# A token-mixing product made from seven products of quarters, in two passes

## The chip, the cores and the metric

One core of one Trainium2 chip runs the whole kernel in one launch. The metric is the device time of that launch in microseconds (us), the median of three runs. A profiled execution gives the trace that the numbers below come from; its own time stands beside its span.

## The reference

```python
def _A_ref(x, wqkv, wo):                 # S=2048, D=512, 32 heads of 16
    q, k, v = ...                        # x @ wqkv, cut in heads
    scores = jnp.einsum("bhqd,bhkd->bhqk", q, k) * scale
    o = jnp.einsum("bhqk,bhkd->bhqd", _softmax(scores), v)
    return o.transpose(0, 2, 1, 3).reshape(B, S, D) @ wo

def _B_ref(x, w_in, w_sp, b_sp, w_out):  # Fh=688
    z = _gelu(jnp.einsum("bsd,df->bsf", x, w_in))
    z1 = z[..., :Fh]
    z2 = _layernorm(z[..., Fh:], axis=-1)
    g = jnp.einsum("ts,bsf->btf", w_sp, z2) + b_sp[None, :, None]
    return jnp.einsum("bsf,fd->bsd", z1 * g, w_out)

h = x + _A_ref(_layernorm(x, axis=-1), A_wqkv, A_wo)
h2 = h + _B_ref(_layernorm(h, axis=-1), B_w_in, B_w_sp, B_b_sp, B_w_out)
```

The change is about `w_sp @ z2`, a 2048 x 2048 matrix by a 2048 x 688 one, and what surrounds it.

## The kernel before

All data are fp32. Every product is made from two parts of each operand, a rounded high part and the rest, both in a reduced fp32 format (`F32R`): `split` (L74-81) makes them, the high part by a copy on ScalarE (ACT), VectorE (DVE) or GpSimd (POOL), the low part by a subtraction on DVE or POOL, and `mm3` (L83-86) issues three matmuls, high by high, high by low, low by high. S is cut into NB = 16 row blocks of 128, the 688 columns of z1 and z2 into two halves of FC = 344, and the 688 rows of w_out into six blocks (five of 128, one of 48).

There are four stages.

1. Up to about 190 us: layer norm, the projection to q, k and v, and their stores.
2. Up to 1422 us: attention, as a loop over 512 units (`units`, L644), whose order on each engine is written by hand. In some units `load_weights` (L629-642) loads a piece of wo or w_in and splits it on POOL. The last units already start the next stage for the first row blocks (`load_o`, `split_o`, `make_h`, L693-698).
3. The middle stage, up to 1594.7 us, in which a scheduler orders the instructions. Per row block: `load_o` (L540) loads the attention's result and scales it on POOL, `split_o` (L554) splits it, `make_h` (L559) multiplies it by wo, adds x, stores h in DRAM and normalises it into `hn` (L573, DVE); `turn` (L724) transposes `hn` into `hT`; `make_z` (L733) makes z1 and z2 by 48 matmuls with w_in, gelu on ACT (L745), stores z1 in DRAM (L748, on SyncE's queue, SP), normalises z2 (L752, DVE) and splits it into the resident operand `z2`, which holds all 16 blocks.
4. The last stage, also ordered by the scheduler. `load_ws` (L709) loads the next row of w_sp blocks (1 MB) and splits it on ACT and DVE. `gate` (L789) makes one row block of g, two halves of 16 x 3 matmuls of 344 columns, then adds b_sp and multiplies by z1 (L803, DVE). `finish` (L807) transposes that product in six blocks (L814), copies them out of PSUM as two parts in groups of two, three and one (`pT`), multiplies by w_out's parts `wu` in 18 matmuls of 512 columns, adds h (L823) and stores the output (L824). `finish` of a block stands behind `gate` of the next one. `load_wu` (L781) loads w_out at the stage's start and splits it on POOL.

SBUF memory comes from pools; tiles with one tag and `bufs=n` share n places, so a new tile waits for the last reader of the one whose place it takes. PSUM has four accumulators `g`, two `acc` and one tile `tp` in the last stage.

Of the kernel before, what the change touches and what calls it, by code (L numbers as in the profile page):

```python
# [18 lines left out]
P = 128  # L19
# [7 lines left out]
NB = S // P  # L27
NQ = S // 512
# [15 lines left out]
def block_kernel(ctx: ExitStack, tc: tile.TileContext, x, wqkv, wo, w_in, w_sp4, b_sp, w_out, out):  # L44
# [26 lines left out]
    z_scr = dram.tile([S, FH], F32, name="z_scr")  # L71
# [458 lines left out]
    wc = ctx.enter_context(tc.tile_pool(name="wc", bufs=3))  # L530
    early = ctx.enter_context(ExitStack())
    ec = early.enter_context(tc.tile_pool(name="early_c", bufs=1))
    e2 = early.enter_context(tc.tile_pool(name="early_2", bufs=2))
    wo2 = [wc.tile([P, DB, D], F32R, name=f"wo{i}", tag="w8") for i in range(2)]
# [24 lines left out]
    def make_h(sb, acc):  # L559
# [12 lines left out]
        hns[sb] = e2.tile([P, D], F32, name="hn")  # L572
        nc.vector.tensor_scalar(hns[sb], h, mv[:, 0:1], rs, op0=ALU.subtract, op1=ALU.mult)  # L573

    with ExitStack() as at:
# [53 lines left out]
        def load_weights(i):  # L629

            t = wc.tile([P, DB * D], F32, name="wg", tag="w8")
# [10 lines left out]
            split(dst[0][:, a, f], dst[1][:, a, f], t, "pool", "pool")  # L642

        units = [(hg, qb, kb) for hg in range(HG) for qb in range(NQ) for kb in range(NB)]  # L644
        prev, turn, later = None, [0], []
        with tc.manual_schedule(engines={E.PE, E.Activation, E.DVE, E.SP}):
            for n in range(0, len(units), 2):
# [43 lines left out]
                if n % 32 == 16 and n < 6 * 32:  # L691
                    load_weights(n // 32)
                if n in (498, 502, 506):  # L693
                    load_o((n - 498) // 4)
                if n in (502, 506):
                    split_o((n - 502) // 4)
                if n in (504, 508):
                    make_h((n - 504) // 4, later[0].tile([P, 512], F32, name="h"))
# [5 lines left out]

    zc = ctx.enter_context(tc.tile_pool(name="zc", bufs=1, side="right"))
    z2 = [zc.tile([P, NB, FH], F32R, name=f"z2{i}") for i in range(2)]
    wsp = [wc]

    def load_ws(tb):  # L709
        pool = wsp[tb % 2]  # L710
        t = pool.tile([P, NB, P], F32, name="wt", tag="w8")
        nc.sync.dma_start(t, w_sp4[tb])
        ws = [pool.tile([P, NB, P], F32R, name=f"ws{i}", tag="w8") for i in range(2)]
        for k in range(2):
            b = slice(k * NB // 2, (k + 1) * NB // 2)
            split(ws[0][:, b, :], ws[1][:, b, :], t[:, b, :], "act")
        return ws

    with ExitStack() as mid:
        m2 = mid.enter_context(tc.tile_pool(name="mid_2", bufs=2))  # L720
        ps = mid.enter_context(tc.tile_pool(name="mid_ps", bufs=5, space=PSUM))
# [11 lines left out]
        def make_z(sb):  # L733
            hT = hTs.pop(sb)
            z = [m2.tile([P, FH], F32, name=f"z{i}") for i in range(2)]
            st = m2.tile([P, 2, 6], F32, name="zst")
            for i in (1, 0):
                for c in range(2):
# [12 lines left out]
            rs = rstd_of(m2, mv[:, 1:2], 1)  # L751
            nc.vector.tensor_scalar(z[1], z[1], mv[:, 0:1], rs, op0=ALU.subtract, op1=ALU.mult)  # L752
# [3 lines left out]
        turn(0)  # L756
        split_o(2)
        for sb in range(NB):
            if sb + 2 < NB:
                make_h(sb + 2, ps.tile([P, 512], F32, name="acc"))  # L760
            if sb + 3 < NB:
                load_o(sb + 3)
                split_o(sb + 3)
            if sb + 1 < NB:
                turn(sb + 1)
            if sb == NB - 2:
                ws = load_ws(0)
            make_z(sb)
# [3 lines left out]
    with ExitStack() as fin:  # L772
        fc_ = fin.enter_context(tc.tile_pool(name="fin_c", bufs=1))
        f2 = fin.enter_context(tc.tile_pool(name="fin_2", bufs=2))
        wsp.append(fin.enter_context(tc.tile_pool(name="fin_w", bufs=3)))
# [3 lines left out]
        wu = [fc_.tile([P, len(FB), D], F32R, name=f"wu{i}") for i in range(2)]  # L779

        def load_wu():  # L781
            t = f2.tile([P, len(FB), D], F32, name="wg", bufs=1)
            nb, fn = len(FB) - 1, FB[-1][1]
            nc.sync.dma_start(t[:, :nb, :], w_out[:nb * P, :].rearrange("(a p) c -> p a c", p=P))
            nc.sync.dma_start(t[:fn, nb, :], w_out[nb * P:, :])
            for i, (_, n) in enumerate(FB):
                split(wu[0][:n, i, :], wu[1][:n, i, :], t[:n, i, :], "pool", "pool")

        def gate(tb, ws):  # L789

            rows = slice(tb * P, (tb + 1) * P)
            z1 = f2.tile([P, FH], F32, name="z1")
            nc.sync.dma_start(z1, z_scr[rows, :])
            g = [ps_g.tile([P, 512], F32, name="g") for i in range(2)]
            for i in range(2):
                f = slice(i * FC, (i + 1) * FC)
                for sb in range(NB):
                    mm3(g[i][:, :FC], ws[0][:, sb, :], ws[1][:, sb, :],
                        z2[0][:, sb, f], z2[1][:, sb, f], sb == 0, sb == NB - 1)
            pr = f2.tile([P, FH], F32, name="pr")  # L800
            for i in range(2):
                f = slice(i * FC, (i + 1) * FC)
                nc.vector.scalar_tensor_tensor(pr[:, f], g[i][:, :FC], bias[:, tb:tb + 1], z1[:, f],  # L803
                                               op0=ALU.add, op1=ALU.mult)
            return pr

        def finish(tb, pr):  # L807
            rows = slice(tb * P, (tb + 1) * P)
            h = f2.tile([P, D], F32, name="h")
            nc.sync.dma_start(h, h_scr[rows, :])  # L810
            pT = [f2.tile([P, len(FB), P], F32R, name=f"pT{i}") for i in range(2)]
            tp = ps_t.tile([P, 8, P], F32, name="tp")
            for i, (f0, fn) in enumerate(FB):
                nc.tensor.transpose(tp[:fn, i, :], pr[:, f0:f0 + fn], ident)  # L814
                if i in (1, 4, 5):
                    b = slice({1: 0, 4: 2, 5: 5}[i], i + 1)
                    split(pT[0][:fn, b, :], pT[1][:fn, b, :], tp[:fn, b, :], "act")
            acc = ps_o.tile([P, 512], F32, name="acc")
            for i, (f0, fn) in enumerate(FB):
                mm3(acc, pT[0][:fn, i, :], pT[1][:fn, i, :],  # L820
                    wu[0][:fn, i, :], wu[1][:fn, i, :], i == 0, i == len(FB) - 1)
            y = f2.tile([P, D], F32, name="y")
            nc.vector.tensor_add(y, acc, h)  # L823
            nc.sync.dma_start(out[rows, :], y)  # L824

        prev = None
        for tb in range(NB):
            nxt = load_ws(tb + 1) if tb + 1 < NB else None
            if tb == 0:
                load_wu()  # L830
            pr = gate(tb, ws)
            if prev is not None:
                finish(tb - 1, prev)
            prev, ws = pr, nxt
        finish(NB - 1, prev)


# [27 lines left out]
```

## Time and profile before

| what | us |
|---|---|
| median of three runs | 1930.77 |
| the runs | 1930.58, 1931.93, 1930.77 |
| the profiled execution's own time | 1930.47 |
| its span, from the first to the last instruction | 1928.7 |

The granted TensorE clock of that execution is 0.998 of full speed over the span. In the profile, PE is TensorE's matmuls and PEld its weight loads; a line number is that of the kernel before; a row of a group has the instructions' count, their busy time and the mean duration in ns, then the engine's idle time ahead of them and what ended it. A row of a stretch has its window, its length, and the busy time and number of instructions of each engine in it, then the clock granted, the busy share of the DMA engines and GB/s. A row of the timeline has the start in us and the duration.

### The profile page before, as it was taken

To read this page: it belongs to the slowest core of one execution; us is meant where nothing else is said; L and a number is where in the kernel's file an instruction comes from. 1 tells how busy PE (TensorE), PEld (TensorE's weight loads), DVE (VectorE), ACT (ScalarE), POOL (GpSimd) and SP (SyncE) were. 2 spreads that over 40 slices of the span, in tenths; PEclk is the share of its full clock that TensorE was granted. 3 is DMA by queue.
4 is the path that set the end of the run, shared out by engine and by line. 5 is a ranking of instruction groups with operands and counts; after the bars stand their busy time and mean duration, and the time that the engine had idled before them with its cause. 6 is when DMAs were issued, how large, how long until landed. Compare 5 with 4: busy or idle time off the path is not lost.

```text
span 1928.7 us, 31977 instructions
## 1 busy us (share of the span) xinstructions
PE 1911.9 (99%) x11800; PEld 1094.2 (57%) x11800; DVE 1444.7 (75%) x2886; ACT 1261.6 (65%) x1590; POOL 139.7 (7%) x201
## 2 busy tenths in 40 slices
PE   9999999999999999999999999999999999999999
PEld 6765444444444344444444444444369999989987
DVE  6487999999999999999999999999358773232231
ACT  3335888888888888888888888888943331111110
POOL 2130000101011000000000000000012222000000
PEclk9999999999999999999999999999999999999999
DMA  5777111211221120111021021000143334232210
GB/s 187 194 190 175 40 24 32 71 24 28 50 53 49 38 40 22 31 37 24 24 53 24 13 51 37 13 13 6 29 118 118 109 119 175 81 109 92 81 66 34
DMA packets 121845, 128.90 MB, mean 67 GB/s; under 512 B 60248, under 2 KB 80744, under 8 KB 118104
## 3 DMA queue, kind: packets, MB, share of 16 engines
q1 hardware_dynamic: 121656, 126.84, 24.4%
q8 instruction: 93, 1.52, 0.3%
q14 instruction: 64, 0.52, 0.1%
q0 software_dynamic: 32, 0.01, 0.0%
HBM read 84.32 MB, written 41.55 MB: 65 GB/s over the span
## 4 chain that ended last, share of the span: by engine, by line
PE 93%; DVE 2%; DMA 1%; ACT 1%; SPq 1%; issue 1%; POOL 0%; ACTq 0%; POOLq 0%; DVEq 0%
PE pv L604 25%; PE m L200 25%; PE s L593 12%; PE acc L84 6%; PE acc L86 5%; PE acc L85 5%; PE g L85 4%; PE g L84 4%; PE g L86 4%; PE tp L814 1%; ACT pt L596 0%; DMA rc<-r_scr 0%; DVE rs_t L101 0%; DMA xr<-in_x 0%; SPq L547 0%
## 5 line engine op out<-in xcount | busy, mean ns | idle before, releaser
L596 ACT ACTIVATE pt<-s 128x1024 f32<-128x1024 f32 x1024 | 993.2, 1030 | 144.5 <-PE s L593 140.5
L205 DVE TENSOR_REDUCE mx<-m 128x1 f32<-128x512 f32 x1511 | 958.7, 684 | 105.2 <-PE m L200 64.7
L200 PE MATMUL m<-kst,qst 48*128 48x512 f32 x1511 | 607.1, 448 | 0.0
L604 PE MATMUL pv<-pt,vst 128*32 128x512 f32 x4096 | 550.7, 605 | 0.4 <-ACT o L611 0.4
L593 PE MATMUL s<-qst,kst 50*128 50x512 f32 x2048 | 465.6, 428 | 2.6 <-ACT pt L596 2.0
L200 PEld LDWEIGHTS m<-kst,qst 48*128 48x128 f32 x1511 | 263.2, 184 | 315.8 <-DVE mx L205 221.7
L593 PEld LDWEIGHTS s<-qst,kst 50*128 50x128 f32 x2048 | 223.2, 185 | 56.8 <-ACT pt L596 32.4
L200 PE MATMUL m<-uvs,qst 48*128 48x512 f32 x503 | 249.0, 496 | 0.0
L200 PEld LDWEIGHTS m<-uvs,qst 48*128 48x128 f32 x503 | 91.8, 183 | 207.3 <-DVE mx L205 205.3
L214 DVE CUSTOM_DVE_ANT_0 ab<-m,ab 128x512 f32<-128x512 f32 x252 | 171.6, 681 | 3.7 <-ACT ab L210 2.0
L604 PEld LDWEIGHTS pv<-pt,vst 128*32 128x32 f32 x4096 | 82.9, 108 | 160.9 <-issue 155.1
L76 ACT ACTIVATE ws<-wt 128x1024 fp32r<-128x1024 f32 x32 | 33.6, 1055 | 210.8 <-PE g L85 203.6
L84 PE MATMUL g<-z,ws 128*128 128x344 f32 x512 | 165.2, 323 | 0.6 <-issue 0.6
L85 PE MATMUL g<-z,ws 128*128 128x344 f32 x512 | 164.7, 322 | 0.0
L86 PE MATMUL g<-z,ws 128*128 128x344 f32 x512 | 163.4, 319 | 0.0
L210 ACT ACTIVATE ab<-m 128x512 f32<-128x512 f32 x251 | 151.0, 602 | 16.7 <-PE m L200 16.3
L803 DVE SCALAR_TENSOR_TENSOR pr<-g,bias,z 128x344 f32<-128x344 f32 x32 | 18.4, 576 | 182.3 <-PE g L86 180.3
L85 PEld LDWEIGHTS g<-z,ws 128*128 128x128 f32 x512 | 96.2, 188 | 5.8 <-issue 5.2
L84 PEld LDWEIGHTS g<-z,ws 128*128 128x128 f32 x512 | 96.2, 188 | 0.9 <-issue 0.9
L86 PEld LDWEIGHTS g<-z,ws 128*128 128x128 f32 x512 | 96.2, 188 | 0.6
L84 PE MATMUL acc<-wi,hT 128*128 128x344 f32 x256 | 83.7, 327 | 0.0
L86 PE MATMUL acc<-wi,hT 128*128 128x344 f32 x256 | 82.4, 322 | 0.0
(136 smaller groups left out, 1603.7 us busy)
## 6 DMA issues: line engine op xcount, KB each, us to landing
wt<-in_w_sp SPq DMA_DIRECT2D x16, 1024.0 KB
qst<-q_scr SPq DMA_DIRECT2D x192, 64.0 KB
kst<-k_scr SPq DMA_DIRECT2D x48, 256.0 KB
k_scr<-part SPq DMA_DIRECT2D x16, 512.0 KB
q_scr<-part SPq DMA_DIRECT2D x16, 512.0 KB
z_scr<-z SPq DMA_DIRECT2D x16, 344.0 KB
z<-z_scr SPq DMA_DIRECT2D x16, 344.0 KB
xg<-in_x SPq DMA_DIRECT2D x16, 256.0 KB
```

The source lines that it names most:

```text
L76: nc.scalar.activation(hi, src, AF.Copy)
L84: nc.tensor.matmul(ps, lh, rh, start=first, stop=False)
L85: nc.tensor.matmul(ps, lh, rl, start=False, stop=False)
L86: nc.tensor.matmul(ps, ll, rh, start=False, stop=last)
L200: nc.tensor.matmul(acc, q[r, p, c], keys[r, p], start=True, stop=True)
L205: nc.vector.reduce_max(at(t, e if t else e - 1), acc, axis=AX.X)
L210: nc.scalar.activation(ab[0], acc, AF.Abs)
L214: nc.vector.tensor_tensor_reduce(ab[0], acc, ab[0], 0.5, LOW, ALU.add, ALU.max, at(0, 0))
L593: nc.tensor.matmul(s[:, t, :], k[r, p, kb * P:(kb + 1) * P], q[r, p, :], start=True, stop=True)
L596: nc.scalar.activation(t, s, AF.Exp, scale=DH ** -0.5)
L604: nc.tensor.matmul(pv[0][32 * j:32 * j + 32, :], vst[hg % 2][:, c:c + 32], pts[j % 2][:, j // 2, :], start=kb == 0, stop=kb == NB - 1)
L814: nc.tensor.transpose(tp[:fn, i, :], pr[:, f0:f0 + fn], ident)
```

## The change

Write w_sp as quarters a11, a12, a21, a22 of eight by eight blocks and z2 as b11, b12, b21, b22 (eight row blocks by 344 columns). In place of eight products of quarters there are seven, on sums and differences:

- s1 = a21 + a22, s2 = s1 - a11, s3 = a11 - a21, s4 = a12 - s2
- t1 = b12 - b11, t2 = b22 - t1, t3 = b22 - b12, n4 = b21 - t2 (as the code has them)
- pass 1: g7 = s3 t3, g6 = s2 t2, g4 = a22 n4, g5 = s1 t1; pass 2: g1 = a11 b11, g3 = s4 b22, g2 = a12 b21

Pass 1 goes over p = 0 to 7, one row of blocks of the upper and the lower half of w_sp at a time. `rows_of_a` loads a11, a21 and a22 of row p, makes the sums on DVE and stores s2; `put` makes the parts; the four products follow; their sums q0, q1, q2 go to DRAM (`g_scr`). It also makes b11's parts, and in its last step those of b22 and b21 and of the first operands of pass 2. Pass 2 goes over p again, with its order on TensorE, ACT and DVE written by hand: three products, which with q give row blocks p (`top`) and p + 8 (`bot`); their transposes, products with w_out and stores stand between the halves of the products. All six transposes of a block are issued ahead of their copies, except for the last block. `fetch` loads what the next step needs.

The operands t3, t2, n4 and t1 are made in the middle stage, on POOL for seven pairs of row blocks and on DVE and ACT for the last; so the row blocks are taken in the order 0, 1, 8, 9, 2, 10, ..., 7, 15. z2 is now stored too, both stores on ACT's queue, and `hn` and z2 are normalised on ACT (`normal`) with a small DVE operation ahead of it.

w_out's parts are made by POOL in six units of the attention (`split_wu`) and stored (`store_wu`); the last step of pass 1 loads them in the places of n4.

The diff, cut:

```diff
+    h_rows = [0, 1, HB, HB + 1] + [sb + HB * i for sb in range(2, HB) for i in range(2)]
...
+    def normal(out, z, mv, rs, pool):
+        nb = pool.tile([P, 1], F32, name="nb")
+        nc.vector.tensor_scalar(nb, rs, mv[:, 0:1], -1.0, op0=ALU.mult, op1=ALU.mult)
+        nc.scalar.activation(out, z, AF.Identity, bias=nb, scale=rs)
...
+        def split_wu(i):
+            f0, fn = FB[i]
+            t = e2.tile([P, D], F32, name="wu", tag="hn", bufs=3)
+            nc.sync.dma_start(t[:fn], w_out[f0:f0 + fn, :])
+            wus[:] = [e2.tile([P, D], F32R, name=f"wu{j}", tag=f"o2{j}", bufs=1) for j in range(2)]
+            split(wus[0][:fn], wus[1][:fn], t[:fn], "pool", "pool")
...
+    def put(slot, halves):
+        op = slot.take()
+        for n in range(2):
+            parts(cut(op[0])[n], cut(op[1])[n], halves[n])
+        return op
...
+    def rows_of_a(p, e):
...
+        load_a(a11, 0, 0, p)
+        load_a(a21, 1, 0, p)
+        load_a(a22, 1, 1, p)
+        combine(e, s3, a11, a21, ALU.subtract)
+        combine(e, a21, a21, a22, ALU.add)
+        combine(e, a11, a21, a11, ALU.subtract)
+        for n in range(2):
+            nc.sync.dma_start(cut(s_scr[p])[n], a11[n])
...
-            nc.sync.dma_start(z_scr[sb * P:(sb + 1) * P, :], z[0])
+            nc.scalar.dma_start(z_scr[0][rows, :], z[0])
...
-            nc.vector.tensor_scalar(z[1], z[1], mv[:, 0:1], rs, op0=ALU.subtract, op1=ALU.mult)
-            split(z2[0][:, sb, :], z2[1][:, sb, :], z[1],
-                  "act" if sb < NB - 1 else None, "pool" if sb < NB - 2 else None)
+            normal(z[1], z[1], mv, rstd_of(m2, mv[:, 1:2], 1), m2)
+            nc.scalar.dma_start(z_scr[1][rows, :], z[1])
...
+            el = "pool" if k < HB - 1 else None
+            e = nc.gpsimd if el else nc.vector
+            (b11, b12), (b21, b22) = ((t[:, :FC], t[:, FC:]) for t in (zs.pop(k), zs.pop(sb)))
+            t2 = m2.tile([P, FC], F32, name="t2", bufs=1)
+            e.tensor_sub(b11, b12, b11)
+            e.tensor_sub(b12, b22, b12)
+            e.tensor_sub(t2, b22, b11)
+            put_t = lambda n, t: parts(T[n][0][:, k, :], T[n][1][:, k, :], t, el, el)
+            put_t("t3", b12)
+            put_t("t2", t2)
+            put_t("t1", b11)
+            e.tensor_sub(b11, b21, t2)
+            put_t("n4", b11)
...
+            if k == NB - 2:
+                raw = rows_of_a(0, nc.vector)
+                ops = {n: put(w[i], raw[n]) for i, n in enumerate(("s3", "s2", "a22"))}
...
+            if not last:
+                raw = rows_of_a(p + 1, nc.vector)
+                nxt["s3"] = put(new[0], raw["s3"])
+                nxt["s2"] = put(new[1], raw["s2"])
...
+                for blocks in (range(HB - 1), range(HB - 1, HB)):
+                    product(g7, ops["s3"], T["t3"], blocks)
+                    product(g6, ops["s2"], T["t2"], blocks)
...
+            nc.scalar.activation(p6, g6, AF.Copy)
+            nc.vector.tensor_add(p67, g7, p6)
...
+            product(g4, ops["a22"], T["n4"])
+            keep(1, g4, p67)
+            if last:
+                wu = [zc.tile([P, HB * FC], F32R, name="wu", tag=f"n4_{i}")[:, :5 * D].rearrange(
+                    "p (a c) -> p a c", c=D) for i in range(2)]
+                for i in range(2):
+                    nc.sync.dma_start(wu[i].bitcast(F32),
+                                      w_scr[i, :5 * P, :].rearrange("(a p) c -> p a c", p=P))
+            product(g5, ops["s1"], T["t1"])
+            keep(2, g5, p67)
+            keep(0, g5, p6)
...
+        prev, nxt = None, fetch(0)
+        with tc.manual_schedule(engines={E.PE, E.Activation, E.DVE}):
+            for p in range(HB):
+                (q, _, z1, h), last = nxt, p + 1 == HB
+                nxt = None if last else fetch(p + 1)
...
+                product(g1, a11, b11, halves[0])
+                if prev:
+                    prev.turn((0, 3), (3, 5), (5, 6))
+                product(g1, a11, b11, halves[1])
...
+                nc.scalar.activation(left, g1, AF.Identity, bias=bt)
+                (nc.gpsimd if p else nc.vector).tensor_mul(bot.pr, bot.pr, z1[1])
+                if not last:
+                    a11 = put(f[0], nxt[1][0])
+                if prev:
+                    prev.multiply(range(len(FB)))
+                product(g3, s4, b22, halves[0])
...
+                nc.vector.tensor_add(right, g3, right)
+                nc.gpsimd.tensor_mul(right, right, z1[0][:, FC:])
+                if not last:
+                    combine(nc.vector, nxt[1][2], nxt[1][1], nxt[1][2], ALU.subtract)
+                    s4 = put(f[1], nxt[1][2])
...
+                product(g2, a12, b21, halves[0])
...
+                if not p:
+                    bot.turn((0, 3), (3, 5), (5, 6))
+                product(g2, a12, b21, halves[1])
+                if not p:
+                    bot.multiply(range(len(FB)))
+                nc.vector.tensor_add(left, g2, left)
+                (nc.vector if last else nc.gpsimd).tensor_mul(left, left, z1[0][:, :FC])
+                if not last:
+                    a12 = put(f[2], nxt[1][1])
...
+                prev = top
+            prev.multiply(range(3, 6), False)
+            prev.turn((0, 3))
+            prev.multiply(range(3))
+            prev.store()
```

More of the change, by code (lines that the diff above doesn't have):

```diff
@@ L27 @@
 NB = S // P
+HB = NB // 2
 NQ = S // 512
@@ new lines, in block_kernel, with __init__, take, parts @@
+    QB = HB // 2
+    class Slot:
+        def __init__(self, pool, tag):
+            self.pool, self.tag = pool, tag
+        def take(self):
+            t = self.pool.tile([P, 2, HB, P], F32R, name="ws", tag=self.tag)
+            return t[:, 0], t[:, 1]
+    def parts(hi, lo, src, el=None, eh=None):
+        if eh == "pool":
+            nc.gpsimd.tensor_copy(hi, src)
+        else:
+            nc.scalar.activation(hi, src, AF.Copy)
+        (nc.gpsimd if el == "pool" else nc.vector).tensor_sub(lo, src, hi.bitcast(F32))
@@ new lines, in rows_of_a @@
+    def rows_of_a(p, e):
+        half = lambda name, tag: e2.tile([P, QB, P], F32, name=name, tag=tag, bufs=3 if tag == "xr" else 2)
+        a11, a21, a22 = ([half(f"a{n}", tag) for _ in range(2)]
+                         for n, tag in ((11, "xr"), (21, "rc"), (22, "o")))
+        s3 = [e2.tile([P, QB, P], F32, name="s3", tag=f"o2{n}", bufs=1) for n in range(2)]
+        load_a(a11, 0, 0, p)
[4 more added lines that the diff above has]
+        combine(e, a11, a21, a11, ALU.subtract)
+        for n in range(2):
+            nc.sync.dma_start(cut(s_scr[p])[n], a11[n])
+        return {"s3": s3, "s2": a11, "a22": a22, "s1": a21}
@@ L789, in gate @@
[L789 to L794, printed above, removed]
-            for i in range(2):
[L796 to L835, printed above, removed]
+        b11 = [bc.tile([P, HB, FC], F32R, name=f"b11_{i}") for i in range(2)]
+        def load_b(i, j, k):
+            t = (f1.tile([P, FC], F32, name="b", bufs=3) if k % 2 else
+                 e2.tile([P, FC], F32, name="b", tag="hn", bufs=3))
+            nc.sync.dma_start(t, z_scr[1][(HB * i + k) * P:(HB * i + k + 1) * P, j * FC:(j + 1) * FC])
+            return t
```

229 lines of the change are left out of this document (181 added, 48 removed).

## The prediction

> **What bounds the kernel now.** I read the head of the page first, then the busy time by stretch, then the tile `g` inside the last stage.
>
> ```profile
> span 1928.7 us, 31977 instructions
> PE 1911.9 (99%) x11800; PEld 1094.2 (57%) x11800; DVE 1444.7 (75%) x2886; ACT 1261.6 (65%) x1590; POOL 139.7 (7%) x201
> PE 93%; DVE 2%; DMA 1%; ACT 1%; SPq 1%; issue 1%; POOL 0%; ACTq 0%; POOLq 0%; DVEq 0%
> ```
>
> TensorE is busy 99% of the span and carries 93% of the chain of waits, so only fewer matmul columns, or idle gaps, can move the end. The stretches (length, then busy time of PE, PEld, DVE, ACT and POOL, granted clock, DMA share, GB/s) show whose time the change touches:
>
> ```profile
> 190.00:424.00 234.00, 233.98 (x1536) 96.30 (x1536) 214.77 (x407) 206.42 (x246) 16.23 (x26) 1.00 0.18 39
> 658.00:892.00 234.00, 233.97 (x1536) 96.10 (x1534) 215.11 (x408) 206.62 (x247) 4.88 (x20) 1.00 0.16 33
> 1422.00:1594.70 172.70, 168.86 (x1000) 159.53 (x997) 134.16 (x395) 57.66 (x112) 39.48 (x26) 0.99 0.39 115
> 1594.70:1912.90 318.20, 318.12 (x1872) 292.91 (x1873) 82.68 (x119) 44.74 (x72) 12.89 (x12) 1.00 0.28 95
> 1912.90:1928.70 15.80, 11.04 (x50) 7.40 (x49) 4.49 (x9) 2.30 (x6) 0.00 (x0) 1.00 0.09 34
> ```
>
> The last stage, 1594.7 to 1928.7, is 334.0 us: its gate part runs TensorE without a gap while DVE is at 26% and the DMA engines at 28%. That spare capacity is what the change spends. The middle stage is fuller: DVE 134.16 of 172.7 us.
>
> **Matmuls removed.** A quarter product is eight blocks of three matmuls of 344 columns, 24 in all. Before, each of the 16 row blocks has 96; after, eight steps have four products (pass 1) and eight have three (pass 2): 8 x 4 x 24 + 8 x 3 x 24 = 1344 in place of 1536, 192 fewer. Their spacing, from a stretch with nothing else on TensorE and one of ten whole blocks (tile `g` alone; the page's ACT and POOL columns are absent here):
>
> ```profile
> 1898.40:1912.80 14.40, 14.31 (x91) 14.31 (x92) 0.57 (x1) 1.00 0.12 38
> 1645.60:1851.40 205.80, 157.43 (x961) 151.20 (x961) 11.52 (x20) 1.00 0.28 94
> ```
>
> 14.40 us hold 91 matmuls and 92 weight loads: 0.1565 to 0.158 us each, taken 0.1575. 192 x 0.1575 = **30.2 us removed**. One block is 205.80 / 10 = 20.58 us, of which 96 x 0.1575 = 15.12 are products and 5.46 the finish (six transposes, 18 matmuls with w_out).
>
> **Finishes and tail.** Old stage: 16 x 15.12 + 14 x 5.46 + 15.8 of tail = 334.2, against 334.0 measured. Placing six transposes together changes the order, not the columns, and TensorE already waits for no copy in these blocks, so I take 5.43 per finish, 15 of them = 81.5. The new tail runs half of the last finish ahead of its last transposes:
>
> ```profile
> L803 DVE SCALAR_TENSOR_TENSOR pr<-g,bias,z 128x344 f32<-128x344 f32 x32 | 18.4, 576 | 182.3 <-PE g L86 180.3
> 1914.53 0.49 PE L814 MATMUL tp<-ident,pr 128*128 128x128 f32 x3
> 1915.05 0.49 ACT L76 ACTIVATE pT<-tp 128x384 fp32r<-128x384 f32 x1 [1.15 <-PE tp L814]
> 1915.58 0.56 DVE L81 TENSOR_TENSOR pT<-tp,pT 128x384 fp32r<-128x384 f32 x1 [1.21 <-ACT pT L76]
> 1916.60 0.40 PE L84 MATMUL acc<-wu,pT 128*128 128x512 f32 x1
> 1916.83 0.40 PE L85 MATMUL acc<-wu,pT 128*128 128x512 f32 x1
> 1925.04 0.69 DVE L823 TENSOR_TENSOR y<-acc,h 128x512 f32<-128x512 f32 x1 [1.91 <-PE acc L86]
> ```
>
> After the last product: two DVE operations (0.58 each), three transposes 0.49, copy 0.49, subtraction 0.56, nine matmuls of 512 columns at the 0.23 between the two starts (2.1), y 0.69, then 1928.7 - 1925.73 = 2.97 for the store: 8.5, with hops between engines **10.2**. New stage without waits: 1344 x 0.1575 + 81.5 + 10.2 = 303.4, against 334.2 by the same count: 30.8 less. The 0.6 by which this exceeds the matmuls' 30.2 rests on the estimated hops, so I keep **30.2** and take finish and tail as even.
>
> **New work beside pass 1.** Each step of 96 matmuls (15.1 us) gives DVE six combines and eight low parts of 128x512, one 128x344 low part, and four 128x344 additions that read PSUM; ACT eight casts of 128x512 and two smaller ones; SP six loads of 256 KB, two stores of 256 KB and four transfers of 172 KB.
>
> ```profile
> L81 DVE TENSOR_TENSOR ws<-wt,ws 128x1024 fp32r<-128x1024 f32 x30 | 38.5, 1290 | 12.6 <-ACT ws L76 12.6
> L823 DVE TENSOR_TENSOR y<-acc,h 128x512 f32<-128x512 f32 x16 | 11.1, 692 | 30.9 <-PE acc L86 30.9
> L76 ACT ACTIVATE o<-o 128x512 fp32r<-128x512 f32 x13 | 8.1, 622 | 6.6 <-POOL o L551 3.9 <-PE acc L85 2.7
> L745 ACT ACTIVATE z<-acc 128x344 f32<-128x344 f32 x64 | 28.2, 456 | 62.2 <-PE acc L86 45.9 <-DMA z_scr<-z 14.9 <-POOL z L81 1.0
> 1600.00:1610.00 10.00, 10.00 (x65) 10.00 (x64) 2.94 (x3) 2.12 (x3) 3.93 (x5) 1.00 1.01 373
> 0.00:190.00 190.00, 184.94 (x862) 130.64 (x862) 128.47 (x281) 73.74 (x116) 35.66 (x49) 1.00 0.70 189
> ```
>
> DVE: 14 x 0.69 + 0.5 + 4 x 0.53 = 12.3 us of 15.1 (81%); 0.69 is the nearest row of 128x512, 0.53 lies between 344 columns at that rate (0.46) and the 0.58 of L803. ACT: 8 x 0.62 + 2 x 0.46 = 5.9. DMA: 2.8 MB in 15.1 us = 185 GB/s, half of the 373 GB/s at which the queue was full, and about the 189 GB/s that the first stage moved at share 0.70. All three fit, so the work costs nothing beyond 0.5 us at the first step; without that cover DVE's rival below sets the price. Pass 2 is lighter: TensorE 3 x 3.78 + 2 x 5.43 = 22.2 us per step, DVE about 12, DMA 3.86 MB (q 0.53, a11, a12 and s2 1.57, z1 0.70, h 0.52, the output 0.52) = 174 GB/s. A few of its results pass DVE and POOL (0.9 us) with 12 matmuls (1.9 us) ahead of their reader; **+1.5** for all (bounds 0 and 4).
>
> **The turn from pass 1 to pass 2** is where I see a real wait. SP issues in order. The loads of w_out's parts overwrite n4, so they wait for the last product that reads it, 24 matmuls (3.8 us) ahead of pass 1's end, and everything behind them on SP waits too: two stores of q, the small rest of w_out, q, z1 and h of step 0, and q, a11, a12, s2, z1, h of step 1: 2.6 + 0.4 + 0.2 + 1.7 + 3.2, some 7 to 8 MB with nothing of pass 2 requested earlier. At 373 GB/s (0.37 MB per us) that is 20 us; s2 of step 1 lands after about 15, or 11 into pass 2. `bot` of step 0 needs q, z1 and w_out about 9 to 11 us into it, nearly as late. Worse, ACT's order is written by hand: its casts of step 1's s4 stand ahead of `bot`'s pT copies, and s4 waits for s2. So pT comes some 10 to 12 us after TensorE wants it, with no other matmul placed ahead of it. What a pause costs besides its length:
>
> ```profile
> 1576.81 0.63 PE L729 MATMUL tp<-ident,hn 128*128 128x128 f32 x4 [1.98 <-DVE hn L573]
> 1577.30:1580.70 3.40, 3.40 (x15) 3.40 (x14) 1.56 (x4) 1.38 (x2) 1.35 (x1) 0.54 0.67 239
> 1581.10:1584.50 3.40, 3.40 (x24) 3.40 (x23) 1.57 (x6) 0.57 (x2) 0.00 (x0) 1.00 0.03 7
> ```
>
> After 1.98 us of idle the granted clock is 0.54 for 3.4 us: 15 matmuls in place of 24, about 1.7 us lost. 11 + 1.7 = **13** (bounds 3, all but the pause hidden, and 20, the whole queue in the path).
>
> **Middle stage.**
>
> ```profile
> L573 DVE TENSOR_SCALAR hn<-xr,mv,rs_u 128x512 f32<-128x512 f32 x16 | 9.6, 602 | 0.1
> L752 DVE TENSOR_SCALAR z<-z,zmv,rs_u 128x688 f32<-128x688 f32 x16 | 12.6, 787 | 1.6
> L78 POOL CAST wu<-wg 128x512 fp32r<-128x512 f32 x5 | 4.0, 814 | 25.1 <-DMA wg<-in_w_out 25.1
> L81 POOL TENSOR_TENSOR z<-z,z 128x688 fp32r<-128x688 f32 x14 | 24.4, 1742 | 24.3 <-ACT z L76 22.3 <-PE acc L86 2.0
> ```
>
> The normalisations (DVE 0.60 and 0.79 per block) go to ACT, which is at 33%; z's stores go to ACT's queue; T needs per pair of rows on POOL eight subtractions and four copies of 128x344. The gelus are on ACT too, so a late ACT queue could hold `hn`; I take the last two blocks only, where DVE has six combines (4.1 us) ahead of the last normalisation: **+1** (bounds -2, the DVE time saved, and +8, both stalls at 1576 growing by a combine chain). T's last entry trails the last matmul by some 4.5 us (gelu, normalisation, subtractions, part); 42 matmuls that don't read it (6.6 us) cover that.
>
> **w_out's parts in attention** cost POOL about 2 us in each of six units. The first two rows of the stretches answer it: with POOL at 16.23 us and at 4.88 us TensorE was equally full, 233.98 and 233.97 of 234. Nothing.
>
> **The sum.** 1928.7 - 30.2 + 1.0 + 0.5 + 13 + 1.5 = 1914.5 of span. The profiled execution took 1930.47, 1.8 more than its span, giving 1916.3; the runs' median is 0.3 above that execution: **1916.5 us**, 0.7% less. Own range 1905 to 1927: the turn at 5 with the middle stage at -2, or the turn at 20 with the middle stage at +4.
>
> **Rivals.** *The turn is hidden* (1906): the queue drains at full rate and DVE and ACT catch up. For it: 373 GB/s was reached beside matmuls. Against: the order on ACT. 13 becomes 3.
>
> *DVE sets pass 1* (1936, slower). Its 81% leaves 2.8 us per step. DVE executes in order, and each put needs an ACT cast just before it, each a21 a load. Idle of more than 4.7 us in each step would lengthen the step to 17 us, and 8 x 1.9 = 15 us turns the sum to no gain; at 17.6 us it is 20 us: 1936. For it: the low parts of `ws` waited 12.6 us for ACT in 30 operations (0.4 each; eight times 0.4 is 3.3). Against: two steps' operands may be in the air, so a late cast need not be paid by TensorE.
>
> *DMA sets it* (1972): below 169 GB/s the gain is gone; at 150 GB/s each pass grows by 28 us. Against it the 189 GB/s of the first stage at share 0.70.
>
> *POOL and DVE block each other in the middle stage* (1951).
>
> ```profile
> L81 DVE TENSOR_TENSOR o<-o,o x13: 681/1489/2220, 1426.9 to 1559.4; 128x512 fp32r<-128x512 f32 x13
> L81 DVE TENSOR_TENSOR hT<-tp,hT 128x512 fp32r<-128x512 f32 x16 | 10.8, 675 | 1.9 <-ACT hT L76 1.8
> ```
>
> The same subtraction takes 0.675 us from PSUM (`hT`) but a median of 1.489 and up to 2.220 with both operands in SBUF (`o`) while POOL works. POOL's work for T is, by the two POOL rows above scaled to 344 columns, 8 x 0.87 + 4 x 0.55 = 9.2 us per pair, in place of 2 x 1.74. If DVE's 17.2 us per pair stood still for half of it, the stage would grow 5 us a pair, 35 in all: 1951. It decides once DVE's idle per block (now 172.7 - 134.2 over 16 = 2.4) is used up. Against it: DVE has one such operation per block left.
>
> By the Trainium skill (SBUF — State Buffer, section "SBUF: two separate sides") the port that DVE and GpSimd share is an exclusive lock: the loser of two operations with SBUF inputs blocks fully. The row of `o` agrees; by that rule each of DVE's subtractions could stand behind one of POOL's whole operations.
>
> **Chances and range.** Forecast 0.57, hidden turn 0.20, DVE 0.13, DMA 0.05, POOL 0.05. A measurement of this kernel tells 0.2% (3.9 us) from no change: the forecast and the hidden turn are faster but for a part of 0.02, and DVE's case reaches no change with 0.05: faster 0.75, same 0.07, slower 0.18. Range 1904 to 1932: it leaves out most of the last two rivals and half of DVE's.
>
> **What would show it.** 1344 matmuls of `g` products at 0.1575; pass 1 at 15.1 us a step with TensorE above 98%; one pause of 8 to 13 us near 13 us into pass 2, released by ACT's pT, which waited for s4; the attention unchanged. Wrong would be pauses in every step of pass 1 that DVE or a load ends, or a middle stage longer than 180 us.

## The result and the profile after

| | before | changed |
|---|---|---|
| median of four runs, us | 1931.35 | 1914.62 (without the longest, 1913.73) |
| runs, us | 1930.58 to 1932.82 | 1911.98, 1913.73, 1915.51 (and 2416.24) |
| span of the profiled execution, us | 1928.7 | 1913.7 |

The run of 2416.24 us had a granted clock of 0.654 from end to end and is left out of the ratio: 0.9908, 95% interval [0.9888, 0.9927]. The changed kernel is 0.9% faster; 1916.5 had been forecast.

The head of the page after, and the share of the chain of waits by engine:

```profile
span 1913.7 us, 32477 instructions
PE 1881.6 (98%) x11608; PEld 1067.1 (56%) x11608; DVE 1532.8 (80%) x3101; ACT 1326.3 (69%) x1729; POOL 215.5 (11%) x293
PE 9%; DMA 2%; DVE 2%; issue 0%; SPq 0%; ACT 0%; DVEq 0%; ACTq 0%
```

There are 192 matmuls fewer (11800 to 11608), and TensorE now idles 32 us in place of 17. The chain covers only the time from about 1654 us on here: at the start of pass 2 it leaves TensorE for the DMA queue, and ahead of that it runs on DVE and its loads. The same kernel by stretches (columns as before: length, PE, PEld, DVE, ACT, POOL, clock, DMA share, GB/s):

```profile
658.00:892.00 234.00, 234.00 (x1536) 96.24 (x1532) 214.81 (x408) 206.69 (x247) 10.60 (x26) 1.00 0.19 43
1422.00:1594.40 172.40, 168.37 (x1003) 158.11 (x1000) 121.25 (x403) 71.47 (x131) 84.89 (x97) 1.00 0.54 163
1594.40:1714.80 120.40, 120.33 (x768) 120.36 (x769) 90.32 (x167) 50.12 (x97) 0.00 (x0) 1.00 0.60 190
1714.80:1903.80 189.00, 173.61 (x941) 151.27 (x940) 96.03 (x167) 47.37 (x101) 32.27 (x22) 0.95 0.54 174
1903.80:1913.70 9.90, 5.47 (x23) 3.32 (x21) 2.28 (x4) 0.49 (x1) 0.00 (x0) 0.94 0.07 26
```

The attention is as full as before, with POOL at 10.60 us for w_out's parts where it had 4.88. The middle stage ends where it did. Pass 1 holds its 768 matmuls with TensorE busy 120.33 of 120.40 us: 0.1568 each. The loss is in pass 2, busy 173.61 of 189.00 at a clock of 0.95, and all of it lies at its start. The chain of waits there, then two rows of its surroundings (the first load of w_out's parts on SP, and DVE's last two additions of pass 1):

```profile
1716.94 1.77 SPq L961
1718.81 0.67 SPq L910
1719.58 9.19 DMA g_scr<-q
1728.85 0.38 SPq L982
...
1730.28 5.08 DMA z<-z_scr
1735.38 7.45 DMA s<-s_scr
1742.92 0.70 DVE s L782
1743.64 0.64 ACT ws L762
...
1745.52 0.80 PE acc L90
...
1783.99 0.65 PE tp L1010 x6
...
1849.28 0.66 PE tp L1010 x6
```

```profile
1714.90 0.39 SPq L961 DMA_DIRECT2D wu<-w_scr  x1
1717.77 0.93 DVE L909 TENSOR_TENSOR q<-g,p 128x344 f32<-128x344 f32 x2
```

A store of q of 172 KB takes 9.19 us; the 2.6 MB of w_out's parts (L961) were issued ahead of it. In the variants below that issue them behind it, it took 4.3 to 6.0 us from its issue to DVE's next start, so they are a large part of it and not all. The memory that step 0's q, z1 and h use comes free only with that store, so SP stands from 1721.3 to 1728.85; then z1 is late, then s2 of step 1, and pT's copies behind s4. DVE has a share too: its last addition for q ended at 1718.70, 3.8 us after pass 2's first product began (1714.86), since the low parts of b22 and b21 stood ahead of it. TensorE's own rows of it, and the clock (column before the DMA share) behind each pause:

```profile
1736.54 1.51 PE L1010 MATMUL tp<-ident,pr 128*128 128x128 f32 x6 [12.11 <-DVE pr L1048]
1744.70 0.50 PE L88 MATMUL acc<-wu,pT 128*128 128x512 f32 x1 [3.22 <-ACT pT L80]
1736.50:1741.50 5.00, 4.95 (x18) 4.49 (x18) 1.98 (x4) 1.21 (x2) 0.56 (x1) 0.50 1.02 353
1745.30:1748.70 3.40, 3.34 (x9) 2.52 (x9) 2.49 (x6) 1.70 (x4) 1.24 (x1) 0.50 0.46 176
```

The two pauses are 15.3 us, and half the clock over 5.0 and 3.4 us costs about 4.2 more.

From there on the steps run evenly: the two groups of transposes in the chain above (both of a `bot`) are three steps apart, 65.29 / 3 = 21.76 us each.

| term of the sum, us | forecast | measured |
|---|---|---|
| middle stage, against its old end at 1594.7 | +1.0 | -0.3 |
| pass 1 | 121.0 + 0.5 | 120.4 |
| products of pass 2 | 576 x 0.1575 = 90.7 | 576 x 0.1568 = 90.3 |
| 15 finishes | 15 x 5.43 = 81.5 | 15 x 5.24 = 78.5 |
| turn and small waits of pass 2 | 13 + 1.5 | 189.0 - 90.3 - 78.5 = 20.2 |
| tail | 10.2 | 9.9 |

A finish is half of what a step of 21.76 us has beside its 72 x 0.1568 us of products; at that spacing the old one was 20.58 - 96 x 0.1568 = 5.53. The middle stage's -0.3 is less than it varies: the other variants with the same middle stage end it between 1593.2 and 1597.9. The forecast's sum had a further 0.4 us in it, since I had not taken the estimated gain of finish and tail.

### The profile page after: what moved, and what is told of

It is laid out like the page before. It is cut to its first block, busy times and chain, and to the rows that moved or that the text cites. A ratio compares the mean times of both kernels' runs of the same rounds, so it can differ in the third digit from the quotient of the medians.

```text
span 1913.7 us, 32477 instructions
## 1 busy us (share of the span) xinstructions
PE 1881.6 (98%) x11608; PEld 1067.1 (56%) x11608; DVE 1532.8 (80%) x3101; ACT 1326.3 (69%) x1729; POOL 215.5 (11%) x293
## 5 line engine op out<-in xcount | busy, mean ns | idle before, releaser
L214 ACT ACTIVATE ab<-m 128x512 f32<-128x512 f32 x251 | 150.9, 601 | 16.8 <-PE m L204 16.3
L82 POOL CAST mparts<-nm 128x16 fp32r<-128x16 f32 x32 | 6.3, 198 | 749.9 <-DVE nm L224 749.9
L762 ACT ACTIVATE ws<-a 128x512 fp32r<-128x512 f32 x80 | 46.6, 625 | 60.8 <-issue 26.7
L88 PE MATMUL acc<-wi,hT 128*128 128x344 f32 x256 | 82.9, 324 | 0.0
L89 PE MATMUL acc<-wi,hT 128*128 128x344 f32 x256 | 81.8, 320 | 0.0
L90 PE MATMUL acc<-wi,hT 128*128 128x344 f32 x256 | 81.8, 319 | 0.0
L763 DVE TENSOR_TENSOR ws<-a,ws 128x512 fp32r<-128x512 f32 x80 | 55.8, 741 | 14.4 <-ACT ws L762 14.4
L88 PE MATMUL g<-b,ws 128*128 128x344 f32 x192 | 65.0, 338 | 0.0
L80 ACT ACTIVATE pT<-tp 128x384 fp32r<-128x384 f32 (+2 forms) x48 | 18.4, 382 | 66.4 <-PE tp L1010 49.0
L88 PE MATMUL g<-t,ws 128*128 128x344 f32 x192 | 61.4, 320 | 0.6 <-issue 0.6
L89 PE MATMUL g<-b,ws 128*128 128x344 f32 x192 | 61.9, 322 | 0.0
```

The source lines that it names most:

```text
L88: nc.tensor.matmul(ps, lh, rh, start=first, stop=False)
L89: nc.tensor.matmul(ps, lh, rl, start=False, stop=False)
L90: nc.tensor.matmul(ps, ll, rh, start=False, stop=last)
L214: nc.scalar.activation(ab[0], acc, AF.Abs)
L762: nc.scalar.activation(hi, src, AF.Copy)
L763: (nc.gpsimd if el == "pool" else nc.vector).tensor_sub(lo, src, hi.bitcast(F32))
```

## The experiments

Each is set against the kernel before on the same chip; the variants ran on three chips, and each has one trace. Where two variants of pass 2 are compared, I use the time from the first to the last product with a part of b, from TensorE's records: 188.8 us in the changed kernel, of which 168.8 are work.

**Six transposes together, alone** (kernel before).

```diff
                 nc.tensor.transpose(tp[:fn, i, :], pr[:, f0:f0 + fn], ident)
+            for i, (f0, fn) in enumerate(FB):
                 if i in (1, 4, 5):
```

> The kernel before, with the six transposes of a finish issued together ahead of their copies and nothing else changed. Theory: in the trace of before the first matmul after a group of transposes comes 0.3 us late, and there are three groups per finish; with one group two of them go, about 0.3 us for each of 15 finishes: 4.5 us less than before, 1926.5. Rival (the prediction's step): the placing changes nothing, 1931 within 2.

Measured: ratio 0.9998 [0.9987, 1.0009]. Ten blocks lie between these two groups:

```profile
1666.16 0.82 PE L814 MATMUL tp<-ident,pr 128*128 128x128 f32 x6
...
1871.85 0.82 PE L814 MATMUL tp<-ident,pr 128*128 128x128 f32 x6
```

205.69 us, as before (205.80). The theory falls: grouping the transposes saves nothing, as the prediction had it.

**The 18 matmuls with w_out unbroken** (kernel before, transposes together). TensorE's order by hand; `turn_out` is `finish` up to its copies.

```diff
-        prev = None
-        for tb in range(NB):
+        with tc.manual_schedule(engines={E.PE}):
+            for tb in range(NB):
...
+                    at = {(0, 9): lambda: hold.append(turn_out(tb - 1, prev)),
+                          (0, 13): lambda: finish(tb - 1, hold[0])}
+                pr = gate(tb, ws, at)
```

> The kernel before, with TensorE's order of the last stage by hand: the six transposes together ahead of g's block 9, twelve matmuls of g, then the 18 matmuls with w_out in one run, then the rest of g, as in pass 2 of the changed kernel. Theory: a finish of the changed kernel is 0.3 us shorter because its 18 matmuls are not mixed with those of g; ten blocks then take 202.9 us in place of 205.8, and the whole 15 x 0.29 = 4.3 us less than before. Rival: the 0.3 us belong to the two passes (their operands, their order of loads), ten blocks stay at 205.8.

Measured: ratio 0.9972 [0.9963, 0.9982], 5.4 us less by the ratio. Ten blocks:

```profile
1656.80 0.81 PE L816 MATMUL tp<-ident,pr 128*128 128x128 f32 x6
...
1859.46 0.81 PE L816 MATMUL tp<-ident,pr 128*128 128x128 f32 x6
```

202.66 us, 0.31 less per block. So the shorter finish of the changed kernel comes from its 18 matmuls standing in one run, where the scheduler had mixed them with g's in several pieces. Which of the things that change with the order costs the time (columns, accumulator, weight loads) no run here separates. This part of the gain needs neither the seven products nor the two passes: by the two ratios the changed kernel is about 12 us faster than this one, not 17.

**ACT's and DVE's order in step 0** (changed kernel): the operands of s4 behind `bot`'s copies.

```diff
-                if not last:
+                if p and not last:
                     combine(nc.vector, raw[2], raw[1], raw[2], ALU.subtract)
                     s4 = put(f[1], raw[2])
...
                 if not p:
                     bot.turn((0, 3), (3, 5), (5, 6))
+                    combine(nc.vector, raw[2], raw[1], raw[2], ALU.subtract)
+                    s4 = put(f[1], raw[2])
```

> The changed kernel, with bot's copies of step 0 of pass 2 ahead of step 1's s4 on ACT and DVE. Theory: the second pause (3.2 us) and the half clock behind it go, the first pause of 12.1 us stays, since q and z1 set it: 3 to 5 us less than the changed kernel, about 1910.5. Rival: the whole queue of loads sets the length of the turn, so what is saved is waited for at step 1 instead: 1914.6 within 1.5.

Measured: ratio 0.9894 [0.9878, 0.9909], 1911.60 us, 3.0 less, the lower end of the theory; pass 2 took 183.1 us, 5.7 less. The second pause is gone and the first stays:

```profile
1736.40 1.51 PE L1010 MATMUL tp<-ident,pr 128*128 128x128 f32 x6 [11.72 <-DVE pr L1048]
1741.45 0.50 PE L90 MATMUL acc<-wu,pT 128*128 128x512 f32 x1 [0.38 <-DVE pT L85]
```

**q and z1 of step 0 ahead of w_out's parts** (changed kernel), and **both edits**.

```diff
+                spare = zc.tile([P, HB * FC], F32, name="spare", tag="n4_0")
+                nc.sync.dma_start(q0, g_scr[0].rearrange("i p c -> p i c"))
+                for i in (1, 0):
+                    nc.sync.dma_start(z0[i], z_scr[0][HB * i * P:(HB * i + 1) * P, :])
+                wu = [load_wu(0, "n4_1")]
...
+        wu.append(load_wu(1, "t1_0"))
```

> The changed kernel, with q and z1 of step 0 in the place of the first part of n4, loaded ahead of w_out's parts, which go to the places of the second part of n4 and of t1. Theory: the first pause (12.1 us) shrinks to under 3 us, but ACT's order still holds pT behind s4, so pT comes when s2 of step 1 has landed, near 17 us after pass 1's end in place of 30: 8 to 12 us less than the changed kernel, 1903 to 1907. Rival (the bytes set it, not their order): under 3 us less, above 1911.5.

> Both edits together. Theory: what is left is the wait for w_out's parts and for step 1's a11, 2 to 5 us: 14 to 17 us less than the changed kernel, 1898 to 1901. Rival (bytes): the loads of step 1 are late instead, above 1908.

Measured: 0.9905 [0.9889, 0.9922] and 0.9898 [0.9881, 0.9914]; pass 2 took 185.3 and 183.6 us. The first kernel's 1913.55 us is the rival's number: its pauses are 5.51 and 5.97 us, where the theory had under 3 for the first. The second's 1911.87 is the rival's too, and the combination is no better than the order on ACT alone. Its rows show why:

```profile
1732.64 1.51 PE L1023 MATMUL tp<-ident,pr 128*128 128x128 f32 x6 [7.31 <-DVE pr L1061]
1740.25 0.57 PE L88 MATMUL acc<-wu,pT 128*128 128x512 f32 x1 [2.82 <-ACT pT L80]
1730.11 1.54 DVE L1059 SCALAR_TENSOR_TENSOR pr<-g,bias,spare 128x344 f32<-128x344 f32 x3 [9.36 <-DMA g_scr<-q]
```

q and z1 were loaded, but `bot`'s own tile still lay in memory that the stores of q hold, and DVE waited 9.36 us for one of them (the last row). At this point the rival, that the bytes set the turn, looked right.

**w_out's parts behind the stores of q.** Both edits, with SP's order by hand for these loads.

```diff
-                wu = [load_wu(0, "n4_1")]
...
-        wu.append(load_wu(1, "t1_0"))
+        man = ExitStack()
+        man.enter_context(tc.manual_schedule(engines={E.SP}))
+        wu = [load_wu(0, "n4_1"), load_wu(1, "t1_0")]
```

> The edits of e6_early_q_pt, and w_out's parts loaded behind the stores of q, so that the memory of the first pass comes free before those loads. Theory (order of the queue): bot's first product is ready near 10 us into pass 2 and the pauses of e6 (7.3 and 2.8 us) fall to 6 us or less in all: 4 us less than e6_early_q_pt. Rival (bytes: the queue is full from 3 us after pass 1's end until 30 us after it): pauses of 9 us or more, merely at other places, within 1.5 us of e6_early_q_pt.

Measured: 0.9894 [0.9878, 0.9911], pass 2 183.4 us.

```profile
1726.77 1.51 PE L1025 MATMUL tp<-ident,pr 128*128 128x128 f32 x6 [2.85 <-DVE pr L1063]
1738.13 0.79 PE L88 MATMUL acc<-wu,pT 128*128 128x512 f32 x1 [6.40 <-ACT pT L80]
1736.47 1.22 ACT L762 ACTIVATE ws<-a 128x512 fp32r<-128x512 f32 x2 [9.98 <-DMA a<-in_w_sp]
```

The first pause shrank by 4.5 us and the second grew by 3.6: the rival's numbers. But what ends it is ACT's order again, now the cast of step 1's a11 (the last row), ahead of pT's copies.

**Step 1's a11 behind the copies too**, then **step 1's operands also behind `top`'s addition on DVE**.

```diff
                     bot.turn((0, 3), (3, 5), (5, 6))
+                    a11 = put(f[0], raw[0])
```

> The edits of e10_q_first, and in step 0 of pass 2 the casts and low parts of step 1's a11 also behind bot's copies. Theory (order on ACT: in e10 ACT stood 10 us at a11's cast, with pT's copies behind it): the second pause of 6.4 us falls under 2 us; what is left is step 1's first product, which waits for a11, 3 to 5 us: 2 to 4 us less than e10_q_first. Rival (bytes): a11 lands no earlier and TensorE waits for it 6 us or more, within 1 us of e10_q_first.

Measured: 0.9895 [0.9878, 0.9912], pass 2 183.3 us; the fourth variant at this length. The pause had moved once more:

```profile
1725.99 1.54 DVE L1061 SCALAR_TENSOR_TENSOR pr<-g,bias,spare 128x344 f32<-128x344 f32 x3 [4.89 <-DMA g_scr<-q]
1728.52 1.51 PE L1025 MATMUL tp<-ident,pr 128*128 128x128 f32 x6 [3.57 <-DVE pr L1063]
1738.71 0.42 PE L88 MATMUL g<-b,ws 128*128 128x344 f32 x1 [0.21 <-ACT ws L762]
1743.22 0.51 DVE L1096 TENSOR_TENSOR pr<-g,pr 128x344 f32<-128x344 f32 x1
1743.80 1.29 POOL L1097 TENSOR_TENSOR pr<-pr,spare 128x344 f32<-128x344 f32 x1 [14.03 <-DVE pr L1096]
1745.15 1.54 PE L1025 MATMUL tp<-ident,pr 128*128 128x128 f32 x6 [3.87 <-POOL pr L1097]
```

The time, 0.6 us less than the variant above, is again the rival's number, and its mechanism is not: TensorE waited 0.21 us for a11, against the rival's 6. It waited for `top`, whose addition stood on DVE behind a11 and s4 of step 1.

```diff
-                    a11 = put(f[0], raw[0])
-                    combine(nc.vector, raw[2], raw[1], raw[2], ALU.subtract)
-                    s4 = put(f[1], raw[2])
...
                 nc.vector.tensor_add(left, g2, left)
...
+                if not p:
+                    a11 = put(f[0], raw[0])
+                    combine(nc.vector, raw[2], raw[1], raw[2], ALU.subtract)
+                    s4 = put(f[1], raw[2])
```

> The edits of e11_a11_late, and in step 0 DVE's addition into top's left half ahead of step 1's operands a11 and s4. In e11 TensorE's second pause (3.87 us) was ended by top's multiplication on POOL, which waited 14 us for that addition, which stood behind step 1's loads on DVE. Theory (order on DVE): that pause goes, pass 2 is 4 to 6 us shorter than in e11_a11_late (183.3 us from the first product with b to the last), 177 to 179. Rival (bytes): step 1's a11 lands at the same time and TensorE waits for it instead, 182 or more.

Measured: 0.9854 [0.9836, 0.9872], the best of all, 1902.53 us. Pass 2 took 173.5 us:

```profile
1716.90:1890.40 173.50, 170.23 (x940) 148.01 (x939) 92.93 (x161) 45.93 (x97) 31.36 (x22) 1.00 0.57 185
1714.00:1744.00 30.00, 26.73 (x154) 23.69 (x153) 14.86 (x29) 7.51 (x16) 1.85 (x2) 1.00 0.97 330
1722.40 1.54 DVE L1061 SCALAR_TENSOR_TENSOR pr<-g,bias,spare 128x344 f32<-128x344 f32 x3 [4.37 <-DMA g_scr<-q]
1730.50 0.50 PE L89 MATMUL acc<-wu,pT 128*128 128x512 f32 x1 [1.27 <-DMA wu<-w_scr]
1735.71 0.43 PE L88 MATMUL g<-b,ws 128*128 128x344 f32 x1 [0.78 <-ACT ws L762]
```

The 30 us around the turn of the variant above, for comparison:

```profile
1713.00:1743.00 30.00, 24.27 (x125) 21.42 (x123) 15.37 (x31) 9.84 (x21) 0.91 (x1) 0.89 0.97 333
```

The loads are the same, the DMA engines are as full in both (0.97, 330 and 333 GB/s), and pass 2 is 9.8 us shorter. Not all of that belongs to the edit. `bot`'s first additions (L1061) came 5.5 us after pass 1's end (1716.9) where they had come 10.6 us after it (1715.4), so that the first pause of 3.57 us didn't occur. The two programs are the same up to that point; in the variant above two steps of pass 1 were 0.7 us longer each, and DVE's last addition for q ended 5.7 us after pass 2's first product began, here 1.1. The first pause cost 3.57 us and about 2.9 for half the clock behind it (TensorE's records show it until 1734.2), 6.4 in all, so about 3.4 us are left for the edit, under the 4 to 6 expected. In time the two variants stand 7.6 us apart, on different chips. Bytes don't set the turn down to this length; what is left waits for w_out (1.27 us), step 1's a11 (0.78) and pT (1.1 us in two pauses).

**Fewer bytes**: as with a11 behind the copies, but five of w_out's six blocks loaded once and split in step 0.

```diff
+        nc.sync.dma_start(wu_raw, w_out[:5 * P, :].rearrange("(a p) c -> p a c", p=P))
...
+                    for i in range(5):
+                        split(wu_big[0][:, i, :], wu_big[1][:, i, :], wu_raw[:, i, :], "act")
```

> The edits of e11_a11_late, and five of w_out's six blocks loaded once as fp32 and split on ACT and DVE in step 0, in place of loading both stored parts: 1.28 MB less in the turn. Rival of e11 (bytes): 1.28 MB at 0.37 MB per us, 3.5 us less waiting for a11, up to 3 us less than e11_a11_late. Theory (order): if the bytes don't bind, no gain, or 1 us more for the split ahead of pT.

Measured: 0.9869 [0.9848, 0.9889], 1906.32 us, 3.8 less than with both parts loaded; pass 2 176.6 us, 6.7 less. That is more than the 3.5 us of the bytes. A part may again be DVE's, whose last addition for q ended 3.4 us after pass 2's first product began, where it had been 5.7. Read with the last one: with the order of that variant fewer bytes do help, and the reordered one is shorter still with all of the bytes.

**DVE's slack in pass 1** (changed kernel, four and eight more operations of 128x512 per step).

```diff
+        for n in range(4 if p else 0):
+            e.tensor_tensor(s3[n % 2], s3[n % 2], a22[n % 2], ALU.max)
```

> The changed kernel, with four more DVE operations of 128x512 on s3 in each of steps 1 to 7 of pass 1 (the output isn't the reference's). Theory of the forecast: DVE has 4 us free per step and its waits for casts and loads are hidden two steps ahead, 2.8 us more change nothing: six steps stay at 90.1 us. Rival (DVE's own waits set the step as soon as it is over 90% busy): 0.5 to 2 us per step, six steps 93 to 102.

> The same with eight more operations, 5.5 us per step (the output isn't the reference's). Both: DVE is now over the 15.05 us of a step. Theory: a step is DVE's busy time alone, 11.2 + 5.5 = 16.7, six steps 100. Rival: its waits come on top, 18 us or more a step, six steps 108 or more.

Measured: 0.998 [0.9969, 0.9991] and 1.0019 [1.0007, 1.0032]. Pass 1 of the two:

```profile
1597.50:1723.00 125.50, 121.78 (x768) 120.40 (x769) 104.63 (x189) 47.76 (x92) 0.00 (x0) 1.00 0.56 178
1593.50:1732.60 139.10, 129.01 (x768) 126.03 (x769) 120.50 (x215) 50.80 (x95) 0.00 (x0) 0.95 0.52 162
```

It grew by 5.1 and 18.7 us, 0.7 and 2.7 per step with them. Six steps from the second on took 93.3 and 104.0 us, where the changed kernel has 90.2. With four operations the theory that nothing changes falls, and the rival's number holds at its lower end, though DVE is busy 83% of the pass and not over 90%. With eight neither fits: DVE is busy 87% of the pass rather than all of it, so its waits come on top, yet a step stays at 17.7 us in the mean and six steps don't reach 108. The first step with them pays most, 1.71 and 4.28 us of pause for ACT's cast behind the lengthened sums of step 1:

```profile
1614.58 0.42 PE L88 MATMUL g<-t,ws 128*128 128x344 f32 x1 [1.71 <-ACT ws L762]
1614.50:1618.00 3.50, 3.16 (x18) 2.88 (x19) 3.50 (x7) 0.55 (x2) 0.00 (x0) 1.00 0.60 167
```

```profile
1613.09 0.65 PE L88 MATMUL g<-t,ws 128*128 128x344 f32 x1 [4.28 <-ACT ws L762]
```

Four operations are 2.7 us of DVE by their duration of 684 ns, and 0.7 of them showed within pass 1: about 2 us of DVE work per step are covered there. The turn pays as well. Pass 2 took 192.9 us with four, 4.1 more than the changed kernel, though nothing in it was changed, and by the ratios the whole is some 14 us longer (what is left beside the 5.1 and 4.1 isn't explained).

Five traces have the loads of the turn in the changed kernel's order (but for two loads of b with eight operations), and in them the first pause goes with how late DVE is. With the end of DVE's last addition for q 1.9, 3.7, 3.8, 5.8 and 6.7 us after pass 2's first product began (t on DVE, below; s4 behind the copies; the changed kernel; eight operations; four), the first pause was 10.1, 11.7, 12.1, 13.2 and 15.3 us. So DVE's work of pass 1, which TensorE doesn't wait for inside the pass, seems to be paid in part at the turn; no run here changes that delay alone.

**The operands t and n4 on DVE and ACT** (changed kernel).

```diff
-            el = "pool" if k < HB - 1 else None
+            el = None
```

> The changed kernel, with the operands t3, t2, n4 and t1 made on DVE and ACT for all eight pairs, and POOL left with the scaling of o. Theory (TensorE bounds the middle stage, POOL and DVE only need to fit): DVE goes from 121 to about 149 us of 172, and the stage stays within 2 us of 172.4; o's subtraction comes back to 0.68 us from a median of 1.51. Rival (POOL and DVE hinder each other at the shared operands): the stage is shorter by 2 us or more.

Measured: 0.9934 [0.9912, 0.9957], not told apart from the changed kernel's 0.9908. The stage ended at 1597.2, and in the variants that share the changed kernel's middle stage between 1593.2 and 1597.9; the rival's stage shorter by 2 us or more didn't come. The subtraction that makes `o`'s low part (min/median/max in ns, then first and last start), in the changed kernel and in this one:

```profile
L85 DVE TENSOR_TENSOR o<-o,o x13: 681/1508/1830, 1427.4 to 1561.7; 128x512 fp32r<-128x512 f32 x13
```

```profile
L85 DVE TENSOR_TENSOR o<-o,o x13: 650/692/1564, 1426.0 to 1566.0; 128x512 fp32r<-128x512 f32 x13
1422.00:1597.20 175.20, 167.66 (x993) 157.12 (x993) 139.54 (x459) 81.31 (x158) 16.70 (x12) 1.00 0.52 159
```

With POOL at 16.70 us the median is 0.69 us; with POOL at 84.89 us it is 0.8 us more. The Trainium skill (SBUF — State Buffer, "SBUF: two separate sides") states that DVE and GpSimd share a port pair under an exclusive lock, on which the loser blocks fully; the two medians agree. No difference shows at the end of the stage in either form: TensorE is busy 168.37 of 172.4 us and 167.66 of 175.2.

## Why the prediction was right, and where its steps were off

**The gain.** The 192 matmuls and their spacing carry it. Pass 1 came out at 120.4 us against 121.5, without a pause of TensorE; this was the claim on which the forecast stood, and the DVE experiments show how narrow the cover was. DVE's rival was the serious one, and it was right in one thing: DVE ended pass 1 3.8 us late, and by the five traces above the turn paid for it.

**The turn: the place right, the main wait another, the size short.** The prediction had one pause of 8 to 13 us, released by ACT's pT, which waited for s4. There were two. The longer one, 12.1 us at `bot`'s first transposes, was ended by DVE's product with z1, whose load SP held back; only the second, 3.2 us, was the one with pT behind s4. Undoing the order on ACT and DVE took 5.7 us off with the half clock behind it. The step that failed in size is the drain of the queue: "At 373 GB/s (0.37 MB per us) that is 20 us; s2 of step 1 lands after about 15, or 11 into pass 2." Its second half landed at 1742.8, 28 us into pass 2. Of the 17 us between, about 4 are in the sum itself: up to s2 the listed loads and stores are some 7.05 MB, 19 us at that rate and not 15. About 4 more are the start: w_out's first load was issued at 1714.90 and not 3.8 us ahead of pass 1's end, because SP stood 6.5 us for DVE with ten loads of b (L886) ahead of it. The remaining 9 or so go with a lower rate of these bytes. In that time SP stood for 7.6 us on memory that the stores of q held, behind w_out's parts: I had counted w_out's wait for n4's place, and not the next loads' wait for the places of pass 1's buffers. The cost was 20.2 us with the small waits, where 13 + 1.5 had been set; 20 had been the bound.

**The finish: a term set at nothing.** "TensorE already waits for no copy in these blocks, so I take 5.43 per finish" was 0.19 us too much per finish, 2.9 in all. Transposes together give nothing, as forecast; what was missed is that order by hand also joins the 18 matmuls, worth 0.31 us a block alone. (The 5.43 also rests on a spacing of 0.1575 where 0.1568 was measured.)

**The tail and the middle stage** were within 0.3 and 1.3 us. The rivals of DMA and of POOL against DVE are out: pass 1 moved 190 GB/s without a pause, and the middle stage kept its length with POOL's work doubled. (The second rival's 1951 was too high by its own rows: DVE's 134.16 us are 16.8 per pair, and half of that less the idle of two blocks, 4.8, is 3.6 and not 5.)

So 1916.5 against 1914.62 is close in part by luck: +5.7 us of turn stood against -3.0 of finishes, -1.1 of pass 1, -1.3 of the middle stage and smaller terms. The terms are less exact than the sum.

## What to carry to other kernels

When a stage is cut in two, the price is paid at the seam: look there for what each in-order engine has ahead of the instruction that TensorE waits for, loads and operands of the next step above all, and for stores that hold memory which the next stage's tiles need. Look too at how late an engine ends that the first stage never waited for: here DVE's 3.8 us. A pause that moves from place to place while its length stays the same looks like a bound of bytes; only following it to the next in-order queue, four times here, told the two apart. In this kernel it paid to keep the 18 matmuls with w_out in one run: mixed with the others they cost 0.31 us more per block.

## What the hardware showed that I had not expected

Breaking up a run of 18 matmuls of 512 columns with others of 344 costs TensorE time though its rows show no idle: 20.58 us a block mixed, 20.27 unbroken. A pause of 1.98 us had halved the clock in the kernel before (0.54); one of 1.71 us, with four more DVE operations, was followed by 3.5 us at 1.00, and so were those of 1.27 and 0.78 us in the best variant. It isn't the length of one pause alone: with eight more operations, pauses of 1.37 and 0.56 us, 0.6 us apart, were followed by half the clock:

```profile
1667.50:1670.90 3.40, 3.40 (x14) 3.40 (x13) 3.39 (x8) 0.00 (x0) 0.00 (x0) 0.50 0.83 251
```

A store of 172 KB took 9.19 us with 2.6 MB of loads ahead of it on the same queue, and 4.3 to 6.0 us in the variants with those loads behind it.
